# Where the routing coefficient enters the early slots of a two-stage MoE kernel, and where its slot count is read

## The chip, the cores and the metric

One NeuronCore of one Trainium2 chip runs the whole program. The metric is device time in microseconds, a median over executions. Three executions of the kernel before gave 831.27, 835.51 and 840.33 us, so the median is 835.51 us. A profiled execution is one more execution, with its own time.

## The reference

Three parts follow one another, in fp32. Sliding-window attention with 32 global tokens per batch (4 batches, 8 heads, 512 + 32 tokens, head size 64) gives 2176 rows `x` of 512 values, which are 17 tiles of 128 tokens. A SiLU MLP (512 to 2048 to 512) follows. Then comes a mixture of 8 experts in which every token goes to its best expert alone:

```
e_idx  = argmax(x @ w_gate);  gate_w = softmax(x @ w_gate)[e_idx]
eom    = sigmoid(x @ w_output_gate)
h      = relu(x[mask] @ w1[e]);  ye = h @ w2[e]          # w1: 512x1024, w2: 1024x512
out[mask] = gate_w * eom[e] * ye
```

So each output row is the expert's product times one number of the token, `gate_w * eom`.

## The kernel before

Matrix products run in fp16 with each fp32 operand split into a high and a low half (three products for one). The weights of the experts are scaled by a power of two per expert before the split; `i12` holds the inverse scales of the 8 `w1` and the 8 `w2` matrices.

**Slots.** The mixture gathers tokens into slots of 128 rows. Slots 0 to 7 are the early slots: one per expert, filled from the first 15 token tiles, so that their routing is known before the MLP has ended. Slots 8 to 20 are late: `last()` (L1154) computes which expert each has, once the last two token tiles are through. Up to 31 slots can be needed; slots 21 to 30 run inside an `If` at the end (L1560), which reads the number of slots from `eidx` into a register of every engine and compares it. Here 21 slots suffice and the body is skipped.

**Routing.** `last()` ends the list of rows to gather (`idg`, L1188), and then, behind that instruction, computes more: `early_coefs()` (L1137), the rows to scatter to (`ids`, L1201), the experts of the late slots (`eidx`, L1208 and L1209) and the coefficient of every slot's row (`cof`, L1221). `early_coefs` does the work of `cof` a second time for the 8 early slots alone, from 15 token tiles: three DVE products (L1140), 15 small matmuls (L1143), three DVE sums (L1146 to L1148), the expert's inverse scale (L1150, L1151) and their product `cce` (L1152).

**The mixture.** `class Moe` works in 4 chunks of 256 hidden columns. In a chunk every slot gets `mm_h` (L1310: x times w1, relu, split into `hb`, a DMA transpose issued on SP that gives `hT`) and `mm_y` (L1346: `hT` times w2 into PSUM `yp`). In chunk 0, ACT writes `yp` times a column of coefficients into the slot's accumulator `ys` (L1362); in chunks 1 to 3, DVE adds `yp` times the column to `ys` (L1364); in chunk 3 a GpSimd (POOL) indirect DMA then scatters the 128 rows to `out` (L1366). The column is `cce` for early slots evicted before `last()` is through (6 of them, `nye=6`), otherwise `cc`, which `coefs(c)` (L1297) builds once per chunk: `gi` is the product of the inverse scales per expert (L1299, L1300), the late slots take `gi` of their expert times `cof` (L1302 to L1305), the early ones `gi` times `cof` (L1308). The chunk's next weights are loaded, measured and converted between the slots (L925, L228, L961, L962).

Late slots are gathered by POOL (L1258, L1287); the even ones are transposed by DMAs on SP's queue (L1260), half of the rest by TensorE (L1291), into the buffers `woh` and `wol`.

**What sets the order.** Each engine runs its instructions in the order that the Tile planner wrote down at build time: it simulates the timeline with a cost model of its own and gives each engine the instruction that is ready first there. `tc.high_priority` and `tc.issue_after(ins)` bias it; `issue_after` puts what its block traces on the engine of `ins` behind `ins` in that engine's order, without a wait for its completion, and says nothing about other engines. The load of the slot count carries no such order before the change.

Of the kernel before, what the change touches and what calls it, by code (L numbers as in the profile page):

```python
# [9 lines left out]
F32 = mybir.dt.float32  # L10
# [4 lines left out]
ACTF = mybir.ActivationFunctionType  # L15
ALU = mybir.AluOpType
# [10 lines left out]
NE = 8  # L27
# [18 lines left out]
NCH = FE // CH  # L46
KJ = CH // 128
NS = 1
ST = NS * NE
NSLOT = 31  # L50
ND = NSLOT - ST
NMAIN = 21
NEARLY = NE
# [54 lines left out]
def tile_kernel(ctx: ExitStack, tc, csa, csr, q0, q, qn, qg, k0, k, va, vc, w_in, w_out, wg, w1, w2, out, dbg=None):  # L108
    nc = tc.nc
# [872 lines left out]
    eidx = const.tile([128, ND + 1], I32, name="eidx")  # L982
    ohs = const.tile([128, ND, NE], F32, name="ohs")
    idge = const.tile([128, NEARLY], I32, name="idge")
    cce = const.tile([128, NEARLY], F32, name="cce")
    bnd = const.tile([128, 1, NE], F32, name="bnd")

    def route(rt, rps):
        def T(shape, name, dt=F32):
            return rt.tile(shape, dt, name=name)  # L990

        def bc(x, shape):
            return x.to_broadcast(shape)
# [24 lines left out]
        RE = ohb[:, 0:15]  # L1018
# [115 lines left out]
                coef(14, 15)  # L1134
                static(0, 15)

        def early_coefs():  # L1137
            SR = [128, 15, NEARLY]
            for c in range(3):
                DVE.tensor_tensor(Rce[:, :, c], RE, bc(cp[:, c, 0:15], SR), ALU.mult)  # L1140
            pc = rps.tile([128, 3, NEARLY], F32, tag="av", name="pce")
            for i in range(15):
                PE.matmul(pc.rearrange("p c n -> p (c n)"), A[:, i], Rce[:, i].rearrange("p c n -> p (c n)"),  # L1143
                          start=(i == 0), stop=(i == 14))
            v = T([128, 1, NEARLY], "ve")
            DVE.tensor_copy(v[:, 0], pc[:, 2])  # L1146
            DVE.tensor_tensor(v[:, 0], v[:, 0], pc[:, 1], ALU.add)
            DVE.tensor_tensor(v[:, 0], v[:, 0], pc[:, 0], ALU.add)  # L1148
            g = T([128, 1, NE], "ge")
            DVE.tensor_tensor(g[:, 0], i12[:, 0:NE], i12[:, NE:2 * NE], ALU.mult)  # L1150
            DVE.tensor_scalar(g, g, 2.0 ** 19, None, ALU.mult)  # L1151
            DVE.tensor_tensor(cce, v[:, 0], g[:, 0], ALU.mult)  # L1152

        def last():  # L1154
            with tc.high_priority(URG):
                p = onehot(15, 17)
# [30 lines left out]
                        pm_i = PE.matmul(pm, A[:, i], Rc[:, i, c], start=(i == 0 and c == 0), stop=(i == NT - 1 and c == 1))  # L1187
                key_i[0] = DVE.tensor_scalar(idg, pm, -1.0, 0.0, ALU.add, ALU.max)  # L1188
            with tc.issue_after(key_i[0].ins):
                early_coefs()  # L1190
                for c in range(2):
                    DVE.tensor_tensor(Rc[:, :, c], R, bc(row[2 + c], SR), ALU.mult)
                pm = rps.tile([128, NSLOT], F32, tag="av", name="pt")
                for i in range(NT):
                    for c in range(2):
                        PE.matmul(pm, A[:, i], Rc[:, i, c], start=(i == 0 and c == 0), stop=(i == NT - 1 and c == 1))
                ohr = oh.rearrange("p i e -> p (i e)")
                vf = ohr[:, 0:2 * NSLOT].rearrange("p (a n) -> p a n", a=2)
                DVE.tensor_scalar(vf[:, 1], pm, 0.0, float(BIG), ALU.is_equal, ALU.mult)
                DVE.tensor_scalar(vf[:, 1], vf[:, 1], -1.0, None, ALU.add)  # L1200
                DVE.tensor_tensor(ids, vf[:, 1], pm, ALU.add)  # L1201

                SE = [128, ND, NE]
                o2 = tmp.rearrange("p i e -> p (i e)").bitcast(BF16)[:, 0:ND * NE].rearrange("p (n e) -> p n e", e=NE)
                DVE.tensor_tensor(o2, bc(bnd, SE), bc(iota[:, 0:ND].rearrange("p (n a) -> p n a", a=1), SE), ALU.is_le)
                ef = T([128, ND, 1], "ef")
                DVE.tensor_reduce(ef[:, :, 0], o2, AX.X, ALU.add)
                DVE.tensor_scalar(eidx[:, 0:ND], ef[:, :, 0], float(NE - 1), None, ALU.min)  # L1208
                DVE.tensor_copy(eidx[:, ND:ND + 1], bnd[:, 0, NE - 1:NE])  # L1209
                DVE.tensor_tensor(ohs, bc(iota[:, 0:NE].rearrange("p (a e) -> p a e", a=1), SE), bc(ef, SE), ALU.is_equal)  # L1210

                coef(15, 17)
                for c in range(3):
                    DVE.tensor_tensor(Rc[:, :, c], R, bc(cp[:, c], SR), ALU.mult)
                pc = rps.tile([128, 3, NSLOT], F32, tag="av", name="pcf")
                for i in range(NT):
                    PE.matmul(pc.rearrange("p c n -> p (c n)"), A[:, i], Rc[:, i].rearrange("p c n -> p (c n)"),
                              start=(i == 0), stop=(i == NT - 1))
                DVE.tensor_copy(vf[:, 0], pc[:, 2])
                DVE.tensor_tensor(vf[:, 0], vf[:, 0], pc[:, 1], ALU.add)  # L1220
                DVE.tensor_tensor(cof, vf[:, 0], pc[:, 0], ALU.add)  # L1221
# [8 lines left out]
    class Moe:  # L1230
        def __init__(self, slots, ne):
            self.slots, self.ne, self.ns = slots, ne, len(slots)
            self.ev, self.x, self.hT, self.ys, self.hb, self.cc = {}, {}, {}, {}, {}, {}
            self.late, self.xg, self.pair = False, [], [None, None]
            for n, x in enumerate(slots):
                if x < ST:
                    self.ev[n] = x // NS
            o = [z for e in range(0, NE, 2) for k in range(NS) for z in (NE * k + e, NE * k + e + 1)] if ne else []
            self.order = o + list(range(len(o), self.ns))
# [54 lines left out]
            else:  # L1294
                DVE.tensor_copy(x, p)

        def coefs(self, c):  # L1297
            g = cc_p.tile([128, 1, NE], F32, tag="gi", name="gi")
            DVE.tensor_tensor(g[:, 0], i12[:, 0:NE], i12[:, NE:2 * NE], ALU.mult)  # L1299
            DVE.tensor_scalar(g, g, 2.0 ** 19, None, ALU.mult)  # L1300
            t = lg.rearrange("p i e -> p (i e)")[:, 0:ND * NE].rearrange("p (n e) -> p n e", e=NE)
            DVE.tensor_tensor(t, ohs, g.to_broadcast([128, ND, NE]), ALU.mult)  # L1302
            cc = self.cc[c] = cc_p.tile([128, NSLOT], F32, tag="cc", name="cc")
            DVE.tensor_reduce(cc[:, ST:], t, AX.X, ALU.add)
            DVE.tensor_tensor(cc[:, ST:], cc[:, ST:], cof[:, ST:], ALU.mult)  # L1305
            for k in range(NS):
                r = slice(k, ST, NS)
                DVE.tensor_tensor(cc[:, r], cof[:, r], g[:, 0], ALU.mult)  # L1308

        def mm_h(self, n):  # L1310
            x = self.x[n]
# [34 lines left out]
        def mm_y(self, c, n):  # L1346
            s = self.slots[n]
            q, o = divmod(n, 2)
            h = self.hT[q][:, 4 * o:4 * o + 4]
            p, tag = ((ps_x, "x2"), (ps_v, "av"))[n % 2]  # L1350
            ps = p.tile([128, DM], F32, tag=tag, name="yp")
            for m, (hl, l) in enumerate(((0, 0), (0, 1), (KJ, 0))):
                for j in range(KJ):
                    PE.matmul(ps, h[:, hl + j], self.rows("2", n, l, j),  # L1354
                              start=(m == 0 and j == 0), stop=(m == 2 and j == KJ - 1))
            if c == 0:
                if n < self.ne:
                    self.ys[n] = ysv[:, n]
                else:
                    self.ys[n] = self.room(n - self.ne, 1)  # L1360
                cc = self.cc[0][:, s:s + 1] if self.late else cce[:, n:n + 1]
                ACT.activation(self.ys[n], ps, ACTF.Copy, scale=cc)  # L1362
            else:
                DVE.scalar_tensor_tensor(self.ys[n], ps, self.cc[c][:, s:s + 1], self.ys[n], ALU.mult, ALU.add)  # L1364
            if c == NCH - 1:
                ins = POOL.indirect_dma_start(out=out[:, :], out_offset=bass.IndirectOffsetOnAxis(ap=ids[:, s:s + 1], axis=0),  # L1366
                                              in_=self.ys[n], in_offset=None, bounds_check=NTOK - 1, oob_is_err=False)
                tc.declare_no_dep(ins.ins, group="sc", reason="every row is written once")
                tc.add_to_no_dep_group("sc", ins.ins)

        def early(self, ny, i0, i1):
            with tc.issue_after(i0.ins):
                for n in range(2, self.ne):
                    self.mm_h(n)
            with tc.issue_after(i1.ins):
                for n in range(ny):
                    self.mm_y(0, n)
# [44 lines left out]
    with ExitStack():  # L1422
# [134 lines left out]
        ys_p = ctx.enter_context(tc.tile_pool(name="ys", bufs=1))  # L1557
        moe.ys_p, moe.late = ys_p, True
        moe.rest(P["nye"], wq1)
    with tc.If(nc.values_load(eidx[0:1, ND:ND + 1], min_val=0, max_val=ND) > NMAIN - ST):  # L1560
        with ExitStack():
            moe = Moe(list(range(NMAIN, NSLOT)), 0)
            moe.ys_p, moe.late = ys_p, True
            wq = [(0, kd, p) for kd in ("1", "2") for p in range(4)]
            while wpend or wq:
                pump_w(wq)
            moe.rest(0, [(1, "1", p) for p in range(4)])
# [48 lines left out]
```

## Time and profile before

| | us |
|---|---|
| median of three executions | 835.51 |
| the profiled execution | 835.75 |
| its span in the trace | 834.0 |
| TensorE busy in the span | 759.4 (91%) |
| DVE busy | 600.4 (72%) |
| ACT busy | 517.7 (62%) |
| mean granted TensorE clock | 0.973 of full |

The span runs from the first instruction to the last. The profile's chain of waits goes back from the last instruction to whatever released it, step by step. A timeline row gives start, duration, engine, line, operation and tiles; the bracket at its end is the idle time of that engine just before, and what ended it. A name of an engine with a `q` behind it is its instruction queue. The last 270 us or so are the mixture, about 63 us for each of the later chunks.

### The profile page before, as it was taken

How to read it: one execution, taken by the hardware profiler on the slowest of the kernel's cores; microseconds unless marked ns; L12 is line 12 of the kernel's file. 1: busy time of each engine (PE TensorE's matmuls, PEld its weight loads, DVE VectorE, ACT ScalarE, POOL GpSimd, SP SyncE). 2: the span in 40 equal slices, each digit the busy share in tenths (PEclk: the TensorE clock that was granted, in tenths of full speed). 3: DMA queues.
4: the chain of work that ended last, by engine and by line, in shares of the span. 5: the costliest groups of instructions: out<-in, count | busy, mean ns of one | idle time of the engine just before them, and what ended most of it. 6: DMA issues, size and time to landing. Idle time of an engine off the chain costs nothing.

```text
span 834.0 us, 17487 instructions
## 1 busy us (share of the span) xinstructions
PE 759.4 (91%) x6249; PEld 527.4 (63%) x6249; DVE 600.4 (72%) x1653; ACT 517.7 (62%) x1020; POOL 56.8 (7%) x110
## 2 busy tenths in 40 slices
PE   6999949899999989989999989998799798998995
PEld 5998726466776757667766656766566465565552
DVE  4799877767966878747755587749364878878863
ACT  3786667867847758646643895342379666856730
POOL 0000000000000000000000000032300000000144
PEclk9999969999999999999999999999999999999998
DMA  9962552658945475744545865075966746955583
GB/s 321 324 196 88 160 167 102 176 114 195 183 110 74 89 130 119 153 77 77 110 62 103 258 202 153 13 188 131 201 134 189 228 83 171 258 109 165 151 186 104
DMA packets 176235, 126.25 MB, mean 151 GB/s; under 512 B 155149, under 2 KB 156941, under 8 KB 172944
## 3 DMA queue, kind: packets, MB, share of 16 engines
q1 hardware_dynamic: 172784, 115.10, 56.7%
q0 software_dynamic: 3360, 9.97, 4.2%
q8 instruction: 54, 0.88, 0.4%
q14 instruction: 37, 0.30, 0.1%
HBM read 76.93 MB, written 9.96 MB: 104 GB/s over the span
## 4 chain that ended last, share of the span: by engine, by line
PE 41%; DMA 12%; DVE 7%; ACT 5%; issue 3%; SPq 1%; POOLq 0%; ACTq 0%; DVEq 0%
PE h L688 9%; PE x L735 9%; PE yp L1354 9%; PE hp L1325 6%; DMA ws<-in_w_dram 5%; DMA pT<-pb 4%; PE hp L1317 2%; PE av L538 2%; DMA wil<-hb 1%; DVE w1b L962 1%; ACT w1b L961 1%; DMA woh<-yx 1%; PE hp L1320 1%; ACT junk L228 1%; ACT w2b L961 1%
## 5 line engine op out<-in xcount | busy, mean ns | idle before, releaser
L735 PE MATMUL x<-woh,g 128*128 128x512 f16 x544 | 172.3, 379 | 3.5 <-ACT g L718 1.5
L688 PE MATMUL h<-xT,wih 128*128 128x256 f16 (+1 forms) x1152 | 160.4, 271 | 10.1 <-DMA xT<-xb 4.9
L735 PEld LDWEIGHTS <-g 128*128 128x128 f16 x816 | 76.4, 98 | 85.3 <-issue 2.7
L688 PEld LDWEIGHTS <-wih 128*128 128x128 f16 x1152 | 108.1, 100 | 34.2 <-DMA xT<-xb 5.2
L1354 PE MATMUL yp<-w2b,wil 128*128 (+1 forms) x384 | 93.7, 391 | 11.0 <-ACT w2b L961 5.3
L735 PE MATMUL x<-wol,g 128*128 128x512 f16 x272 | 103.1, 379 | 0.0
L688 PE MATMUL h<-xT,wil 128*128 128x256 f16 (+1 forms) x576 | 88.0, 272 | 0.0
L690 ACT ACTIVATE tanh<-h,th 128x512 f32<-128x512 f32 (+1 forms) x72 | 47.2, 658 | 64.0 <-PE h L688 61.4
L470 ACT ACTIVATE e<-e,mx,esc 128x192 f32<-128x192 f32 (+1 forms) x128 | 70.1, 549 | 18.5 <-DVE mx L467 15.5
L1354 PEld LDWEIGHTS <-wil 128*128 128x128 f16 x384 | 38.1, 103 | 51.4 <-DMA wil<-hb 8.4
L707 ACT ACTIVATE g<-tanh,i_out 128x512 f16<-128x512 f32 (+1 forms) x64 | 44.1, 691 | 33.3 <-DVE tanh L703 33.2
L228 ACT ACTIVATE junk<-ws 128x1024 f16<-128x1024 f32 x48 | 50.4, 1052 | 17.4 <-DMA ws<-in_w_dram 17.2
L466 DVE CUSTOM_DVE_ANT_0 e<-s,cs 128x192 f32<-128x192 f32 (+1 forms) x128 | 42.5, 367 | 23.2 <-PE s L455 10.4
L688 PEld LDWEIGHTS <-wil 128*128 128x128 f16 x576 | 54.4, 100 | 7.4 <-issue 0.5
L708 DVE SCALAR_TENSOR_TENSOR g<-tanh,i_out,g 128x512 f16<-128x512 f32 (+1 forms) x64 | 45.6, 713 | 17.0 <-ACT g L707 16.9
L703 DVE SCALAR_TENSOR_TENSOR tanh<-tanh,h 128x512 f32<-128x512 f32 (+1 forms) x64 | 41.4, 649 | 21.3 <-ACT tanh L690 21.0
L962 DVE SCALAR_TENSOR_TENSOR w1b<-ws,s,w1b 128x1024 f16<-128x1024 f32 x32 | 40.4, 1280 | 17.2 <-ACT w1b L961 17.0
L1325 PE MATMUL hp<-w1b,x 128*128 128x256 f16 x384 | 48.7, 279 | 1.2 <-ACT r L1338 1.2
L1325 PEld LDWEIGHTS <-x 128*128 128x128 f16 x384 | 38.6, 102 | 10.7 <-issue 2.1
L523 DVE SCALAR_TENSOR_TENSOR pb<-e,pb 128x384 f16<-128x384 f32 (+1 forms) x48 | 27.6, 586 | 22.9 <-ACT pb L522 22.8
L962 DVE SCALAR_TENSOR_TENSOR w2b<-ws,s,w2b 128x1024 f16<-128x1024 f32 x32 | 40.2, 1280 | 2.6 <-ACT w2b L961 2.6
L1364 DVE SCALAR_TENSOR_TENSOR yx<-yp,cc,yx 128x512 f32<-128x512 f32 x39 | 29.1, 748 | 8.9 <-PE yp L1354 8.8
(361 smaller groups left out, 1447.6 us busy)
## 6 DMA issues: line engine op xcount, KB each, us to landing
ws<-in_w_dram SPq DMA_DIRECT2D x64, 512.0 KB, 4.5
st<-in_w_out_dram SPq DMA_DIRECT2D x8, 1024.0 KB, 5.0
st<-in_w_in_dram SPq DMA_DIRECT2D x6, 1024.0 KB, 12.0
q<-in_q_dram SPq DMA_DIRECT2D x12, 512.0 KB, 4.0
x2d<-x2s SPq DMA_DIRECT2D x17, 256.0 KB, 2.7
st<-in_k_dram SPq DMA_DIRECT2D x3, 1088.0 KB, 7.0
st<-in_qn_dram SPq DMA_DIRECT2D x3, 1024.0 KB, 5.1
st<-in_va_dram SPq DMA_DIRECT2D x3, 1024.0 KB, 6.9
```

Source lines behind the costliest of these rows:

```text
L228: ACT.activation(junk, x, ACTF.Square, accum_out=m)
L466: DVE.tensor_tensor_reduce(dst[:, hh, 0:wt], ps[:, hh, 0:wt], mask, 1.0, -3e38, ALU.add, ALU.max, mx[:, hh:hh + 1])
L470: ACT.activation(dst[:, hh, 0:wt], dst[:, hh, 0:wt], ACTF.Exp, scale=esc[:, b:b + 1], bias=mx[:, 2 + hh:3 + hh], accum_out=sums[i][:, h:h ...
L688: PE.matmul(ps[:, f], w[:, kk, c], xj[:, l + kk, 0:n], start=(m == 0 and kk == 0), stop=(m == 2 and kk == KD - 1))
L690: pin[0] = ACT.activation(t, ps, ACTF.Tanh, scale=th[:, b:b + 1])
L703: pin[1] = DVE.scalar_tensor_tensor(t, t, 1.0, ps, ALU.add, ALU.mult)
L707: ACT.activation(hi, t, ACTF.Copy, scale=i)
L708: pin[2] = DVE.scalar_tensor_tensor(lo, t, i, hi, ALU.mult, ALU.subtract)
L735: PE.matmul(x2ps[2 * j + c], x[:, f, o], w[:, ff], start=(ff == 0 and m == 0), stop=(ff == KF - 1 and m == 2))
L962: DVE.scalar_tensor_tensor(d[:, 1], t[a], sc_, d[:, 0], ALU.mult, ALU.subtract)
L1325: PE.matmul(ps[:, 0], x[:, xl + kk], self.rows("1", n, l, kk), start=(m == 0 and kk == 0), stop=(m == 2 and kk == KD - 1))
L1354: PE.matmul(ps, h[:, hl + j], self.rows("2", n, l, j), start=(m == 0 and j == 0), stop=(m == 2 and j == KJ - 1))
```

## The change

`early_coefs` and `cce` are gone. A new method `scales` makes `gi` alone, and `early` calls it for chunk 0. Early slots are evicted with their column of `gi` in every chunk; after chunk 3's addition one ACT instruction per early slot multiplies `ys` by the slot's column of `cof` in place, and the scatter follows. `coefs` makes the columns of the late slots only. The load of the slot count is put behind the last scatter in POOL's order.

```diff
         with tc.issue_after(key_i[0].ins):
-                early_coefs()
...
-        def coefs(self, c):
-            g = cc_p.tile([128, 1, NE], F32, tag="gi", name="gi")
+        def scales(self, c):
+            g = self.gi[c] = cc_p.tile([128, 1, NE], F32, tag="gi", name="gi")
             DVE.tensor_tensor(g[:, 0], i12[:, 0:NE], i12[:, NE:2 * NE], ALU.mult)
             DVE.tensor_scalar(g, g, 2.0 ** 19, None, ALU.mult)
+
+        def coefs(self, c):
+            if c not in self.gi:
+                self.scales(c)
+            g = self.gi[c]
...
-            for k in range(NS):
-                r = slice(k, ST, NS)
-                DVE.tensor_tensor(cc[:, r], cof[:, r], g[:, 0], ALU.mult)
...
-                cc = self.cc[0][:, s:s + 1] if self.late else cce[:, n:n + 1]
+                cc = self.gi[0][:, 0, n:n + 1] if n < self.ne else self.cc[0][:, s:s + 1]
                 ACT.activation(self.ys[n], ps, ACTF.Copy, scale=cc)
             else:
-                DVE.scalar_tensor_tensor(self.ys[n], ps, self.cc[c][:, s:s + 1], self.ys[n], ALU.mult, ALU.add)
+                cc = self.gi[c][:, 0, n:n + 1] if n < self.ne else self.cc[c][:, s:s + 1]
+                DVE.scalar_tensor_tensor(self.ys[n], ps, cc, self.ys[n], ALU.mult, ALU.add)
+            if c == NCH - 1 and n < self.ne:
+                ACT.activation(self.ys[n], self.ys[n], ACTF.Copy, scale=cof[:, s:s + 1])
             if c == NCH - 1:
                 ins = POOL.indirect_dma_start(out=out[:, :], ...)
...
+                self.end = ins
 
         def early(self, ny, i0, i1):
+            self.scales(0)
...
-    with tc.If(nc.values_load(eidx[0:1, ND:ND + 1], min_val=0, max_val=ND) > NMAIN - ST):
+    with tc.issue_after(moe.end.ins):
+        more = nc.values_load(eidx[0:1, ND:ND + 1], min_val=0, max_val=ND)
+    with tc.If(more > NMAIN - ST):
```

## Rows read from the trace of the kernel before

**Rows 1.** The page's head.
```profile
span 834.0 us, 17487 instructions
```

**Rows 2.** The page's chain of waits, shares of the span by engine.
```profile
PE 41%; DMA 12%; DVE 7%; ACT 5%; issue 3%; SPq 1%; POOLq 0%; ACTq 0%; DVEq 0%
```

**Rows 3.** Timeline of the end, all engines: start, duration, engine, line, operation.
```profile
822.86 0.75 DVE L1364 SCALAR_TENSOR_TENSOR yx<-yp,cc,yx 128x512 f32<-128x512 f32 x1 [0.55 <-PE yp L1354]
823.88 0.97 POOL L1366 DMA_INDIRECT out_dram<-yx,ids  x1 [0.33 <-DVE yx L1364]
824.15 0.75 DVE L1364 SCALAR_TENSOR_TENSOR yx<-yp,cc,yx 128x512 f32<-128x512 f32 x1 [0.54 <-PE yp L1354]
829.54 0.97 POOL L1366 DMA_INDIRECT out_dram<-yx,ids  x1 [4.68 <-DMA out_dram<-yx,ids]
```

**Rows 4.** Line 1560: durations in ns (min/median/max), first and last start.
```profile
L1560 SPq TENSOR_LOAD <-eidx x1: 1665/1665/1665, 586.0 to 586.0; - x1
...
L1560 ACTq COMPARE_BRANCH  x1: 50/50/50, 811.9 to 811.9; - x1
...
L1560 ACTq EVENT_SEMAPHORE  x1: 17/17/17, 815.7 to 815.7; - x1
...
L1560 PEldq COMPARE_BRANCH  x1: 3807/3807/3807, 821.1 to 821.1; - x1
L1560 POOLq TENSOR_LOAD <-eidx x1: 487/487/487, 823.6 to 823.6; - x1
...
L1560 POOLq COMPARE_BRANCH  x1: 45/45/45, 824.2 to 824.2; - x1
...
L1560 POOLq INC_SWDGE_SEM  x1: 579/579/579, 828.1 to 828.1; - x1
```

**Rows 5.** Line 1366, the scatters: from issue to landing.
```profile
DMA to landing us min/median/max: 2.5/3.3/6.0
```

**Rows 6.** Line 1612, the program's end, on POOL's queue.
```profile
L1612 POOLq DRAIN  x3: 40/113/3825, 829.3 to 833.7; - x3
```

**Rows 7.** Timeline around the end of the routing, all engines.
```profile
575.96 2.75 PE L1354 MATMUL yp<-w2b,wil 128*128 128x512 f16 x12
...
581.13 0.15 DVE L1152 TENSOR_TENSOR cce<-ve,ge 128x8 f32<-128x8 f32 x1
...
581.38 1.26 ACT L1362 ACTIVATE wih<-yp,cce 128x512 f32<-128x512 f32 x2 [1.59 <-DVE gw L1075]
...
582.58 1.47 PE L1354 MATMUL yp<-w2b,wil 128*128 128x512 f16 x6 [2.64 <-ACT wih L1362]
...
594.15 0.93 PE L1325 MATMUL hp<-w1b,woh 128*128 x5 [3.96 <-DMA woh<-yx]
...
594.88 2.76 PE L1354 MATMUL yp<-w2b,wil 128*128 128x512 f16 x6
...
598.68 1.03 PE L1317 MATMUL hp<-w1b,woh 128*128 x4
```

**Rows 8.** The chain of waits in order of time: start, duration, what.
```profile
584.29 9.73 DMA woh<-yx
...
795.80 5.96 DMA wil<-hb
```

**Rows 9.** Stretches: length, busy time of each engine, granted clock, DMA share.
```profile
590.20:594.10 3.90, 0.00 (x0) 0.04 (x1) 0.85 (x2) 0.80 (x2) 2.37 (x3) 1.00 1.04 173
...
594.70:598.20 3.50, 3.50 (x16) 1.74 (x15) 0.00 (x0) 0.51 (x1) 0.00 (x0) 0.51 1.04 221
```

**Rows 10.** The same view in chunk 3, early slots' last additions (PE, PEld, DVE, ACT, POOL).
```profile
786.00:801.00 15.00, 14.23 (x90) 8.57 (x88) 14.52 (x34) 6.77 (x15) 8.76 (x8) 1.00 0.59 144
```

**Rows 11.** Groups by line and shape: busy us, mean ns of one.
```profile
L1362 ACT ACTIVATE wih<-yp,cce 128x512 f32<-128x512 f32 x6 | 4.0, 686 | 11.9 <-PE yp L1354 10.3 <-DVE gw L1075 1.6
L1140 DVE TENSOR_TENSOR ohs<-ohb,cp 128x120 bf16<-128x120 bf16 x3 | 0.7, 279 | 0.0
L1308 DVE TENSOR_TENSOR cc<-cof,gi 128x8 f32<-128x8 f32 x4 | 0.6, 158 | 0.0
L1364 DVE SCALAR_TENSOR_TENSOR wih<-yp,cc,wih 128x512 f32<-128x512 f32 x24 | 16.9, 743 | 0.8 <-PE yp L1354 0.8
```

More of the change, by code (lines that the diff above doesn't have):

```diff
@@ L984, in tile_kernel @@
     idge = const.tile([128, NEARLY], I32, name="idge")
-    cce = const.tile([128, NEARLY], F32, name="cce")
     bnd = const.tile([128, 1, NE], F32, name="bnd")
@@ L1135, in early_slots @@
                 static(0, 15)
[L1137 to L1152, printed above, removed]
         def last():
@@ L1232, in __init__ @@
             self.slots, self.ne, self.ns = slots, ne, len(slots)
-            self.ev, self.x, self.hT, self.ys, self.hb, self.cc = {}, {}, {}, {}, {}, {}
+            self.ev, self.x, self.hT, self.ys, self.hb, self.cc, self.gi = {}, {}, {}, {}, {}, {}, {}
             self.late, self.xg, self.pair = False, [], [None, None]
```

## The prediction

> **What bounds the kernel now.** I read the page first. The span is 834.0 us [rows 1], and the profiled execution took 835.75, so 1.75 us lie outside the span; its time stands 0.24 us above the median of 835.51. Sums are made against 835.75. The chain of waits [rows 2] belongs to PE for 41%, then to DMA (12%): TensorE sets the pace, broken by short stretches in which it waits for something. So an edit is worth what it does at a stretch where PE waits, or at the very end. I then looked at the three places that the change touches.
>
> **The end.** In the timeline [rows 3] each late slot's addition on DVE is followed by its scatter on POOL. The last but one ends at 822.86 + 0.75 = 823.61 and its scatter starts at 823.88, 0.27 later. The last addition ends at 824.90, yet its scatter starts at 829.54. The reader is to see that 4.4 us are lost there, and the trace names a DMA for it. Line 1560's rows [rows 4] show more: POOL's load of the slot count stands at 823.6, its branch at 824.2, and POOL's next instruction at 828.1, 3.9 us on, 0.58 long. So POOL's queue went through the load and the `If` before it took the last scatter. The gap is not POOL's alone: ACT has 3.8 us from its branch (811.9) to its next instruction (815.7), and PE's branch lasts 3.81.
>
> **The routing's end.** In [rows 7] PE finishes two early slots' y products (12 matmuls) and later waits 2.64 us, until 582.58, for ACT's evictions, which began at 581.38 because `cce` came at 581.13. Then PE waits again, 3.96 us until 594.15, for the transposed rows of a late slot: that DMA is on the chain for 9.73 us from 584.29 [rows 8] and the DMA engines are full there (share 1.04, [rows 9]). Behind that wait stand, in PE's order, the y products of the sixth early slot (594.88, 6 matmuls) and at 598.68 the first h products of slot 9, which TensorE had transposed itself and which needs no such DMA.
>
> **Chunk 3, early slots.** From 786 to 801 DVE is busy 14.52 of 15 us, ACT 6.77 [rows 10]: DVE is full, ACT has 8.2 us free.
>
> **The change, part by part.** *Load behind the last scatter.* Moved are POOL's load, and through its register the branch and what follows. The last scatter starts 0.27 behind the last addition: 824.90 + 0.27 = 825.17 instead of 829.54. The load now starts when the queue has passed that scatter, about 824.9 (before: 823.6, as the last but one was released at 823.61). With the distances of [rows 4], branch 0.6 later at 825.5, next instruction 3.9 later at 829.4, 0.58 long: 830.0. Before, POOL's drain ended at 829.3 + 3.8 = 833.1 [rows 6], 3.6 behind the start of the last scatter and 0.9 ahead of the end. Now that scatter allows 825.17 + 3.6 = 828.8, so the branch comes last: 830.0, plus up to 0.6 as between 828.7 and the drain's start at 829.3, plus 0.9 is 831.2. **Gain 2.8 us.** Bounds: if the branch cost nothing the whole 4.4 comes back; if the scatter takes the longest landing of [rows 5], 6.0 instead of the median 3.3, it ends 2.7 later, at 831.5, and the span at 832.4, gain 1.6. I take 2.8, since four engines' distances are the nearest rows. [...] The loads of the other four engines are not tied to anything: SP's, 1.67 us long at 586.0 among the late slots' transposes [rows 4], may stay or go. The transposes there wait on full DMA engines, so I count 0, with 1.7 as its bound either way.
>
> *No `cce`.* Removed from DVE are 3 products of 0.28 and six small instructions of about 0.16 [rows 11], some 1.8 us (`gi` was made before as well), and 15 small matmuls. They stand ahead of `cce` and delay nothing else that PE waits for. What counts is the wait for `cce`: `gi` depends on the weights alone, so ACT can evict the first y product when it ends, near 577.5, and PE's 2.64 us go. What is late next is the DMA that lands at 594.0; nothing here brings it forward. So PE arrives sooner and waits longer, and the gain is only the work that moves from behind 594.15 to ahead of it. The sixth early slot's y products wait for nothing new and are the likeliest: 6 of the 12 matmuls of 2.75 us at 575.96, at full clock, so **1.4 us**, which I take. Low end 0 (order unchanged). [...]
>
> [...]
>
> *Columns.* `coefs` loses one DVE instruction of 0.16 us in each chunk, and the 24 additions of early slots [rows 11] wait for `gi` alone. In chunk 3 DVE is full, so 0.16 may count; I take 0, bounds 0 and 0.6 gained. *Eight multiplications on ACT.* Each is like L1362's, 0.69 us [rows 11] (reading SBUF, not PSUM, so an estimate): 5.5 us in all. They lie between an addition on DVE and a scatter on POOL. Behind them on ACT stand the relu copies and `hb` halves of late slots. ACT's 8.2 free us cover them, and early scatters end 20 us ahead of the last one: I take 0. Low 0, high 5.5 with no cover.
>
> Sum: 835.75 - 2.8 - 1.4 = **831.5 us**.
>
> **Rivals.** *A, PE's second wait fills.* With buffers free sooner, slot 9 and 11 run ahead of slot 10. For it: they need no SP transposes. Against: PE's order is fixed at build, and the order of before left them behind. [...]
> *B, the routing's end gives nothing.* The 2.64 us are moved into the wait at 594. For it: DMA share 1.04. [...]
> *C, slower: ACT takes DVE's lateness.* The place is ACT's order from 786 to 801. A multiplication that waits for a DVE addition holds the `hb` halves behind it, their transposes on SP, and so the y products of late slots, for which PE already waits on a 5.96 us transpose [rows 8]. It decides from the point where ACT's free 8.2 us no longer fall between additions. Price up to 5.5: 835.75 - 2.8 + 5.5 = 838.5, slower than before.
> *D, the move does nothing*, because POOL's `If` is still planned ahead of that scatter: against it, the branch needs the register that the moved load fills. 834.4.
>
> **Numbers.** Chances: forecast 0.47, A 0.2, B 0.17, C 0.13, D 0.03. A measurement of this kernel tells about 1% from no change, 8.4 us here: faster means under 827.2, slower over 843.9. A reaches the first line only at its end, and a re-planned order may add a little: 0.17. Beyond the other line only C with a worse order lies: 0.07. Same: 0.76. The range takes A's end and nearly C's: 826.5 to 838.
>
> **What would show it.** The last scatter 0.3 us behind the last addition, and POOL's branch behind it; the span's end some 6 us behind the last addition, not 9. No PE wait for ACT near 580; the sixth early slot's products ahead of the wait for the late slot's rows. ACT idle between 786 and 801 still over 2 us, and PE's wait for the transpose there no longer than before. I am wrong if the end moves by less than 1.5 us, if PE's waits between 576 and 600 sum to as much as before with the same work left, or if that transpose comes later by more than 2 us.

## The result, and the profile after

The changed kernel takes 826.49 us (median of 6 runs, 825.20 to 828.53); the kernel before, run on the same chip beside it, 837.32. The ratio is 0.988 [0.984, 0.992], a gain of 1.2%, some 10 us. (The ratios leave out runs that were disturbed, so here and below they are not quite the quotients of the medians; the profile of e_nopin is of such a run.) The forecast was 831.5, a gain of 4.2 us by its sum: the sign is right, the size is not, and the time lies at the very edge of the range, whose lower end was 826.5. So the question is where the other 6 us came from.

The profiled execution took 825.91. The page's head and its chain of waits, which answer to [rows 1, 2]:

```profile
span 824.1 us, 17447 instructions
...
PE 43%; DMA 10%; DVE 5%; ACT 4%; issue 4%; POOL 0%; SPq 0%; POOLq 0%; ACTq 0%; DVEq 0%
```

The span is 9.9 us shorter. To see where, I cut both traces at four events that both have: the first `pm` product of the routing, TensorE's last y product of chunk 0, its last one of chunk 1, its last one of chunk 3, and then the stretch from the end of the last addition on DVE. The stretches of before (from:to and length; busy us of PE, PEld, DVE, ACT, POOL with instructions; granted clock; DMA share; GB/s):

```profile
575.10:643.40 68.30, 61.26 (x493) 39.83 (x491) 36.23 (x113) 42.24 (x76) 12.91 (x13) 0.98 0.81 174
643.40:699.70 56.30, 51.80 (x312) 30.43 (x311) 44.38 (x100) 37.77 (x65) 0.00 (x0) 0.97 0.60 160
699.70:824.10 124.40, 113.44 (x702) 69.38 (x700) 96.50 (x219) 70.13 (x127) 19.66 (x20) 0.97 0.69 170
824.90:834.00 9.10, 0.00 (x0) 0.00 (x0) 0.00 (x0) 0.00 (x0) 0.97 (x1) 0.61 0.13 49
```

The same of after:

```profile
575.40:641.00 65.60, 60.80 (x479) 39.38 (x477) 34.98 (x101) 42.31 (x76) 13.08 (x13) 0.97 0.84 180
641.00:699.30 58.30, 52.91 (x310) 30.62 (x310) 45.89 (x105) 38.01 (x66) 0.00 (x0) 0.94 0.66 164
699.30:816.60 117.30, 110.57 (x703) 67.83 (x700) 94.24 (x213) 74.54 (x133) 20.76 (x20) 1.00 0.70 177
817.40:824.10 6.70, 0.00 (x0) 0.00 (x0) 0.02 (x1) 0.00 (x0) 0.97 (x1) 0.70 0.18 66
```

The reader is to see that the third row holds most of it: chunks 2 and 3 take 7.1 us less for the same 702 or 703 matmuls. In that row PE is busy 2.9 us less and idle 4.2 us less (124.40 - 113.44 = 11.0 against 6.7). The end gives 2.4, the routing 2.7, and chunk 1 takes back 2.0.

**The end.** After's timeline (start, duration, engine, line, operation), which answers to [rows 3]:

```profile
816.67 0.75 DVE L1348 SCALAR_TENSOR_TENSOR yx<-yp,cc,yx 128x512 f32<-128x512 f32 x1 [0.54 <-PE yp L1337]
817.70 0.97 POOL L1352 DMA_INDIRECT out_dram<-yx,ids  x1 [0.33 <-DVE yx L1348]
```

The last scatter starts 0.28 us behind the last addition (817.42), where before it was 4.64. The rows of the `If` in after (ns min/median/max, first and last start), which answer to [rows 4]:

```profile
L1550 POOLq EVENT_SEMAPHORE  x4: 17/43/2412, 818.2 to 818.4; - x4
...
L1550 ACTq COMPARE_BRANCH  x1: 50/50/50, 803.1 to 803.1; - x1
...
L1550 ACTq EVENT_SEMAPHORE  x1: 17/17/17, 806.3 to 806.3; - x1
...
L1550 POOLq COMPARE_BRANCH  x1: 45/45/45, 818.0 to 818.0; - x1
...
L1550 POOLq INC_SWDGE_SEM  x1: 595/595/595, 820.9 to 820.9; - x1
```

POOL's branch now stands behind the last scatter, and 2.8 us lie between it and POOL's `INC_SWDGE_SEM` (`INC` from here on). But 2.41 of them are a wait on a semaphore, from 818.44 to 820.85. The chain of before says for what (start, duration, what):

```profile
823.88 4.69 DMA out_dram<-yx,ids
828.57 0.10 POOLq L1560
```

By it, POOL's queue waits there until the scatter that it had issued last has landed. The landing signals themselves agree: the last one of that scatter comes at 828.07 in the trace and `INC` starts at 828.10; in after the last scatter's comes at 820.83 and the wait ends at 820.85. (The chain's 828.57 already lies inside `INC`.) Of before, I had read the 3.9 us behind POOL's branch as the price of the branch, because ACT (3.8 us) and PE (3.81) show as much at theirs.

**The routing's end.** PE's timeline in after, which answers to [rows 7]:

```profile
576.22 2.75 PE L1337 MATMUL yp<-w2b,wil 128*128 128x512 f16 x12
...
579.67 1.46 PE L1337 MATMUL yp<-w2b,wil 128*128 128x512 f16 x6
584.25 1.25 PE L1198 MATMUL pcf<-wil,A 128*128 128x93 bf16 x17 [3.12 <-DVE wil L1195]
585.29 4.12 PE L1337 MATMUL yp<-w2b,wil 128*128 128x512 f16 x12
...
590.08 1.46 PE L1337 MATMUL yp<-w2b,wil 128*128 128x512 f16 x6
...
594.57 1.23 PE L1308 MATMUL hp<-w1b,woh 128*128 x8 [1.68 <-DMA woh<-yx]
```

PE no longer waits for ACT, and all six early slots stand ahead of the wait for the late slot's rows. But it now waits 3.12 us for the operand of the coefficients' product, a wait of 0.4 us before.

**Chunks 2 and 3.** PE's timeline of before around the first y product of chunk 3:

```profile
767.89 1.47 PE L1325 MATMUL hp<-w1b,x 128*128 128x256 f16 x12 [0.69 <-ACT r L1338]
771.99 0.83 PE L1354 MATMUL yp<-w2b,wil 128*128 128x512 f16 x2 [2.63 <-ACT w2b L961]
...
775.19 2.03 PE L1325 MATMUL hp<-w1b,x 128*128 128x256 f16 x15
```

And of after:

```profile
768.81 1.47 PE L1308 MATMUL hp<-w1b,x 128*128 128x256 f16 x12 [0.63 <-ACT r L1321]
771.63 1.47 PE L1337 MATMUL yp<-w2b,wil 128*128 128x512 f16 x6 [1.35 <-DMA wil<-hb]
...
773.23 1.02 PE L1300 MATMUL hp<-w1b,woh 128*128 x4
```

Before, PE comes to slot 0's y product too early and waits 2.63 us for the chunk's weights, which ACT is still converting; chunk 2 has the same wait, 2.66. The stretches behind the two waits in before:

```profile
710.80:714.20 3.40, 3.40 (x18) 2.42 (x17) 1.16 (x6) 2.68 (x5) 0.00 (x0) 0.50 1.00 356
...
772.20:775.60 3.40, 3.14 (x10) 1.31 (x9) 3.14 (x10) 2.53 (x7) 0.00 (x0) 0.50 0.98 377
```

And in after behind the waits that stand there now, 1.22 and 1.35 us:

```profile
711.00:714.40 3.40, 3.40 (x19) 1.71 (x18) 3.20 (x10) 2.22 (x6) 0.00 (x0) 1.00 1.27 257
...
771.60:775.00 3.40, 3.37 (x19) 1.78 (x20) 3.25 (x10) 3.00 (x7) 0.00 (x0) 1.00 1.07 291
```

The granted clock (column before the DMA share) was 0.50 for 3.4 us behind each wait of before, and stays at 1.00 in after. By an estimate from these rows, half of 3.4 us, that is up to 1.7 us lost twice. PE's busy time, which holds this loss, is 2.9 us less in after; the 4.2 us of idle time are the rest of the 7.1.

Why does PE come later to that product? The two programs differ in the order that was written out for TensorE, in places that the diff doesn't touch (h3.5 is the h product of slot 5 in chunk 3, y3.0 the y product of slot 0 there):

```
before  h3.3 h3.4 h3.5 y3.0 h3.6 h3.7 h3.8 y3.2 ...
after   h3.3 h3.4 h3.5 h3.6 h3.7 y3.0 h3.8 h3.9 y3.2 ...
before  ... h2.13 h2.14 h2.15 y2.8
after   ... h2.15 h2.16 h2.17 h2.18 h2.19 h2.20 y2.8
```

The h products of slots 6 and 7 stand ahead of slot 0's y product and fill the time in which its weights are made. The late slots' first y product moved behind the last h product, in chunks 1 and 2.

The first of these two is not enough by itself. Three of the kernels below (e_nocce, e_col, e_force8) have slot 0's y product behind slot 7's h products in chunk 2, but in chunk 1 slot 8's y product begins where before has it. Their chunk 2 takes 63.2 to 64.2 us, as in the kernels with before's order (63.1 to 63.8) and not as in those with after's (60.4 to 61.3). They wait in another place: for `tot`, a small product with which the next weights' size is measured (L192, from ACT's L228), 2.3 to 3.7 us, with half clock behind it (in e_col 0.50 for 3.4 us, from 709.5). e_col's row, and after's in the same place:

```profile
707.88 0.38 PE L192 MATMUL tot<-mw,cr 128*128 128x2 f32 x2 [2.26 <-ACT junk L228]
...
704.49 0.38 PE L192 MATMUL tot<-mw,cr 128*128 128x2 f32 x2 [0.86 <-ACT junk L228]
```

So by these runs the gain of a chunk needs the new order of its own start together with that of the late y products of the chunk before. e_force8's chunk 3, which has both by hand (of the late slots only slot 8's is held), has the gain. Why both are needed is not shown beyond that wait.

### The profile page after: what moved, and what is told of

The parts are those of the page before. It is cut to its first block, busy times and chain, and to the rows that moved or that the text cites. A ratio compares the mean times of both kernels' runs of the same rounds, so it can differ in the third digit from the quotient of the medians.

```text
span 824.1 us, 17447 instructions
## 1 busy us (share of the span) xinstructions
PE 758.7 (92%) x6234; PEld 526.8 (64%) x6234; DVE 598.7 (73%) x1640; ACT 522.3 (63%) x1028; POOL 58.4 (7%) x110
## 4 chain that ended last, share of the span: by engine, by line
PE 43%; DMA 10%; DVE 5%; ACT 4%; issue 4%; POOL 0%; SPq 0%; POOLq 0%; ACTq 0%; DVEq 0%
PE x L735 10%; PE h L688 10%; PE yp L1337 10%; PE hp L1308 5%; DMA ws<-in_w_dram 3%; DMA pT<-pb 3%; PE hp L1300 2%; PE av L538 2%; DMA wil<-hb 2%; PE hp L1303 1%; ACT w1b L961 1%; DMA woh<-yx 1%; DVE w1b L962 1%; ACT junk L228 1%; DMA yx<-x2d,idg 1%
## 5 line engine op out<-in xcount | busy, mean ns | idle before, releaser
L470 ACT ACTIVATE e<-e,mx,esc 128x192 f32<-128x192 f32 (+1 forms) x128 | 70.1, 549 | 18.3 <-DVE mx L467 15.4
L228 ACT ACTIVATE junk<-ws 128x1024 f16<-128x1024 f32 x48 | 50.5, 1052 | 17.6 <-DMA ws<-in_w_dram 17.6
L521 POOL MEMSET pb<- 128x256 f16 (+1 forms) x48 | 12.4, 258 | 328.6 <-DMA pT<-pb 143.6
```

The costliest lines, as they stand in the source:

```text
L228: ACT.activation(junk, x, ACTF.Square, accum_out=m)
L470: ACT.activation(dst[:, hh, 0:wt], dst[:, hh, 0:wt], ACTF.Exp, scale=esc[:, b:b + 1], bias=mx[:, 2 + hh:3 + hh], accum_out=sums[i][:, h:h ...
```

## The experiments

Each ratio is against the kernel before, run on the same chip beside it. There were three chips: e_pin, e_nocce, e_gicol and e_nopin on the first (before there: 839.07), e_wait, e_force8, e_noscale and e_col on the second (845.67), the rest on the third (843.93). The forecasts in us were made against 837 to 839 for the kernel before and 826.5 for after, so on the slower second chip they are to be read as ratios.

**e_pin: the load alone.** The kernel before, with only this:

```diff
-    with tc.If(nc.values_load(eidx[0:1, ND:ND + 1], min_val=0, max_val=ND) > NMAIN - ST):
+    with tc.issue_after(moe.end.ins):
+        more = nc.values_load(eidx[0:1, ND:ND + 1], min_val=0, max_val=ND)
+    with tc.If(more > NMAIN - ST):
```

> The kernel before with one edit: the load of the slot count put behind the last scatter in POOL's order. Theory 1 (the end is worth what the trace after shows: 9.1 us from the last addition to the end of the span before, 6.7 after; the other 7.5 us of the change come from elsewhere): the last scatter starts 0.3 us behind the last addition, the span ends 6 to 7 us behind that addition, and the time is 2.4 us under the kernel before's (837.3), 834.9; the mixture's PE waits stay as before. Rival (moving the load also re-plans the order and is the source of most of the change): under 831.

835.94 us, ratio 0.9995 [0.9955, 1.0036]. Its trace shows the mechanism in full: the last scatter 0.27 us behind the last addition, the span's end 6.6 behind it, not 9.1. Its ratio doesn't show it: 2.4 us are 0.3%, and the interval is 0.4% to each side. So the end term stands by the trace, and the load alone is not what made the kernel faster by 1.2%.

**e_nocce: no `cce` alone.** The kernel before, chunk 0 by `gi`, chunks 1 to 3 by `cc`, no multiplications on ACT:

```diff
-                early_coefs()
...
-                cc = self.cc[0][:, s:s + 1] if self.late else cce[:, n:n + 1]
+                cc = self.gi[0][:, 0, n:n + 1] if n < self.ne else self.cc[0][:, s:s + 1]
```

> The kernel before without early_coefs and cce: the first additions of the early slots (chunk 0) use the inverse scales alone, chunks 1 to 3 use the columns of cc as before, there is no multiplication at the end and the load of the slot count is not moved. The early slots' output lacks the coefficient in chunk 0's part. Theory 1 (removing cce re-plans TensorE's order in chunks 2 and 3 as well, so that it no longer waits 2.6 us before the first y products there and the clock no longer falls): 5 to 7.5 us under the kernel before (837.3), 830 to 832, with two stretches of half clock instead of four in the mixture. Theory 2 (those chunks gain because the additions of early slots wait for gi and not for cc): only the routing's end gains, 1 to 2.5 us, 835 to 836, and four stretches of half clock.

830.69 us, ratio 0.9932 [0.9886, 0.9978]. That is Theory 1's time without its mechanism: TensorE's order of chunk 3 is exactly before's, and chunks 2 and 3 take 124.5 us in the trace, with a half-clock stretch in each (granted clock 0.97 over both, as in before). Near 580 PE waits 3.0 us for the operand of the coefficients' product, in place of the wait for ACT. Where the 0.7% come from the trace does not show.

**e_gicol: the columns alone.** The kernel before, `cce` kept:

```diff
-                DVE.scalar_tensor_tensor(self.ys[n], ps, self.cc[c][:, s:s + 1], self.ys[n], ALU.mult, ALU.add)
+                DVE.scalar_tensor_tensor(self.ys[n], ps, self.gi[c][:, 0, n:n + 1] if n < self.ne else self.cc[c][:, s:s + 1], self.ys[n], ALU.mult, ALU.add)
```

> The kernel before with the early slots' additions of chunks 1 to 3 taking the inverse scales alone as their column; cce stays for chunk 0, the load is not moved, nothing is multiplied at the end. The early slots' output lacks the coefficient in the parts of chunks 1 to 3. Theory 1 (order re-planned by the removal of cce): no gain, 836 to 838. Theory 2 (the wait for cc is what chunks 2 and 3 lost): 4 to 6 us under the kernel before (837.3), 831 to 833.

838.27 us, ratio 1.0005 [0.9953, 1.0057]: that early additions wait for `gi` alone gains nothing by itself that shows at 0.5%.

**e_nopin: the change without the moved load.** The kernel after, with the load where it was:

```diff
-    with tc.issue_after(moe.end.ins):
-        more = nc.values_load(eidx[0:1, ND:ND + 1], min_val=0, max_val=ND)
-    with tc.If(more > NMAIN - ST):
+    with tc.If(nc.values_load(eidx[0:1, ND:ND + 1], min_val=0, max_val=ND) > NMAIN - ST):
```

> The changed kernel with the load of the slot count left where the planner puts it. Theory 1: the last scatter stands behind the If again, 4 us behind the last addition, the span ends 9 us behind it, 2.4 us over the changed kernel (826.5): 829. Rival (the planner puts the load behind the last scatter by itself once the order has changed): 826.5.

829.27 us, ratio 0.988 [0.975, 1.001]; the interval is wide, from 4 runs. In its trace the last scatter is 3.5 us behind the last addition again and the end 8.0. With e_pin: most of the gain is not at the end.

**e_wait: the wait for `cce` put back.** The kernel after, in which the first six evictions take their scale from a copy that DVE makes only behind the routing's `ids`:

```diff
+            with tc.issue_after(i2.ins):
+                DVE.tensor_scalar(cce, self.gi[0][:, 0], 1.0, None, ALU.mult)
...
-                cc = self.gi[0][:, 0, n:n + 1] if n < self.ne else self.cc[0][:, s:s + 1]
+                cc = cce[:, n:n + 1] if n < P['nye'] and self.ne else self.gi[0][:, 0, n:n + 1] if n < self.ne else self.cc[0][:, s:s + 1]
```

> The changed kernel with the wait for the routing put back without its work: the first evictions of the six early slots take a copy of the inverse scales that DVE makes behind the list of rows to scatter to. TensorE's order in chunks 2 and 3 is that of the changed kernel. Theory O (the change gains through TensorE's order in chunks 2 and 3: the first y product there stands behind the h products of slot 7, not of slot 5, and slot 8's behind all h products): PE waits 2 to 3 us for an eviction near 580 again, and the time is within 2 us of the changed kernel's 826.5. Theory M (the eviction wait in the routing was worth most of it): 831 or more.

833.67 us, ratio 0.984 [0.977, 0.990]. PE waits for ACT again (13.6 us, on a chip where other kernels wait as long there for something else, see the last section), and the kernel gains as much as the change. That fits a wait worth nothing, within 0.6%. It is a weak test, though: on this chip PE stands for 12.6 and 13.6 us near 580 also in e_noscale and e_col, which lack the wait that was put back, so that wait can be hidden in the longer stop.

**e_noscale: no multiplications at the end.** The kernel after without these lines:

```diff
-            if c == NCH - 1 and n < self.ne:
-                ACT.activation(self.ys[n], self.ys[n], ACTF.Copy, scale=cof[:, s:s + 1])
```

> The changed kernel without the eight ACT multiplications in chunk 3; the early slots' output lacks the coefficient. TensorE's order is the changed kernel's but for chunk 3's end. Forecast in the prediction: they cost 0, so 826 to 827. Rival C of the prediction (ACT holds the late slots' halves): up to 5.5 us faster, 821 to 824.

836.58 us, ratio 0.986 [0.978, 0.993], no better than e_wait beside it, which has them. With these two intervals the times alone could hardly show 5.5 us (0.65%); what the trace of after says of the multiplications stands in the next section.

**e_col: the columns put back.** The kernel after, in which early additions take their scale from `cc` again, by one DVE instruction in each chunk:

```diff
+            if self.ne:
+                DVE.tensor_tensor(cc[:, 0:ST], cr[:, C_ONE:C_ONE + NE], g[:, 0], ALU.mult)
...
-                cc = self.gi[c][:, 0, n:n + 1] if n < self.ne else self.cc[c][:, s:s + 1]
+                cc = self.cc[c][:, s:s + 1]
```

> The changed kernel with the early slots' column of chunks 1 to 3 copied into cc by one DVE instruction per chunk, as before, so that their additions wait for it. TensorE's order in chunk 3 falls back to that of the kernel before, in chunk 2 half. Theory O: half of the gain of those chunks is lost, 3 to 5 us over the changed kernel, 829.5 to 831.5. Rival (the order there is worth nothing, and 0.16 us per chunk is all): 826.5 to 827.2.

841.29 us, ratio 0.995 [0.992, 0.998]: more than half of the gain is lost, more than Theory O's half, for one small instruction in each chunk. Its program has before's order in chunk 3, and the old wait with it (PE's timeline):

```profile
773.88 0.63 PE L1339 MATMUL yp<-w2b,wil 128*128 128x512 f16 x2 [2.64 <-ACT w2b L961]
...
777.06 4.79 PE L1310 MATMUL hp<-w1b,x 128*128 128x256 f16 x24
```

**e_force8: the kernel before, its order changed by hand in chunks 2 and 3.** Slot 0's y product is held behind slot 7's h product, and slot 8's behind the last h (`hi[n]` is the last h matmul of slot n):

```diff
-                                self.mm_y(c, n)
+                                held = {0: self.hi[7], 8: self.hi[self.ns - 1]}.get(n) if self.ne and c > 1 else None
+                                with tc.issue_after(held.ins) if held else ExitStack():
+                                    self.mm_y(c, n)
```

> The kernel before, with cce, cc and the load as they were, and one thing ordered: in chunks 2 and 3 slot 0's y product stands behind slot 7's h products on TensorE and slot 8's behind the last slot's. Theory O: 5 to 8 us under the kernel before (839 over its many runs), 831 to 834; the 2.65 us waits ahead of the first y products are under 1.5 us. Theory M, or columns: no gain, 837 to 840.

842.22 us, ratio 0.995 [0.991, 0.999]: part of the gain from order alone, and less than Theory O's forecast. Chunk 1 was still planned as in before; chunk 2 takes 64.2 us and keeps its half-clock stretch (719.1; granted clock 0.99 over chunks 2 and 3), behind a wait of 3.73 us for `tot`. Chunk 3, ahead of which slot 8's y product was held too, takes 57.5 us, where before has 61.2 and after 56.9.

**e_full: before's arithmetic in after's order.** The kernel before with e_pin's load and

```diff
+                                held = None if not (self.ne and c) else self.hi[7] if n == 0 else self.hi[self.ns - 1] if n >= self.ne and c < 3 else None
+                                with tc.issue_after(held.ins) if held else ExitStack():
+                                    self.mm_y(c, n)
```

> The kernel before with cce, cc and its four columns untouched, and two orders given by hand: on TensorE, in chunks 1 and 2 every late slot's y product stands behind the last slot's h products, and in chunks 1 to 3 slot 0's y product behind slot 7's h products; on POOL, the load of the slot count stands behind the last scatter. TensorE's order of h and y products from chunk 2 on is then that of the changed kernel. Theory O (the order on TensorE and the end are the whole gain): a ratio to the kernel before of 0.985 to 0.991, as the changed kernel. Rival D (the data flow matters: early columns that wait for nothing but the inverse scales): 0.993 to 0.996, as the runs that had the order or the end only in part.

838.21 us, ratio 0.992 [0.988, 0.996]. This lies between the forecasts of Theory O and rival D, and the interval reaches into both; the trace decides. `cce`, the columns and the coefficients are all as before; h and y products stand as in after in chunk 2 and in chunk 3 up to slot 4's y product. The stretch of chunks 2 and 3:

```profile
712.90:830.10 117.20, 109.98 (x703) 68.05 (x700) 94.99 (x217) 69.41 (x125) 18.90 (x18) 1.00 0.71 178
```

**e_colf: e_col in the same order by hand.** Both edits on the kernel after:

```diff
+                DVE.tensor_tensor(cc[:, 0:ST], cr[:, C_ONE:C_ONE + NE], g[:, 0], ALU.mult)
...
+                held = None if not (self.ne and c) else self.hi[7] if n == 0 else self.hi[self.ns - 1] if n >= self.ne and c < 3 else None
```

> The changed kernel with the early columns of chunks 1 to 3 copied into cc, which alone gave 0.9947, and TensorE's order given by hand as in the last kernel. Theory O: the gain comes back, 0.985 to 0.990. Rival D: it stays at 0.993 to 0.996.

834.65 us, ratio 0.987 [0.982, 0.992], Theory O's and below rival D's: what e_col lost comes back with the order, its extra instructions still there. Its stretch of chunks 2 and 3, ahead of it e_col's:

```profile
701.40:828.70 127.30, 116.85 (x705) 70.44 (x703) 96.78 (x216) 75.78 (x135) 17.62 (x18) 0.96 0.64 166
```

```profile
705.60:823.70 118.10, 110.40 (x703) 67.98 (x700) 94.24 (x216) 74.78 (x133) 18.80 (x18) 1.00 0.69 174
```

**e_after: the change again**, on the third chip, unedited.

> The changed kernel once more, beside the others on their chip. Both theories: 0.984 to 0.992 of the kernel before.

833.39 us, ratio 0.989 [0.984, 0.994].

**e_aft8: after, with slot 8's y product behind the last h in chunk 3 too.** e_force8's edit on the kernel after:

```diff
+                held = {0: self.hi[7], 8: self.hi[self.ns - 1]}.get(n) if self.ne and c > 1 else None
```

> The changed kernel with slot 8's y product of chunks 2 and 3 behind the last slot's h products; only chunk 3 changes by it. Theory O says nothing of this place; if y products that stand ahead of h products wait there for DMA transposes, 0 to 2 us under the changed kernel, otherwise the same within 1 us; the last h products' transposes come earlier, so no loss is expected.

835.37 us, ratio 0.991 [0.986, 0.996]: no better than after. None of these kernels is faster than after by more than the intervals allow.

The length of the stretch of chunks 2 and 3 in all profiles, us, by the order of its program:

| order of chunks 2 and 3 | kernels | us | granted clock |
|---|---|---|---|
| slot 0's first y product in chunk 3 as in before | before, e_pin, e_gicol, e_nocce, e_col | 124.4, 125.7, 123.2, 124.5, 127.3 | 0.97, 0.95, 0.97, 0.97, 0.96 |
| slots 0 and 8 held by hand | e_force8 | 121.8 | 0.99 |
| as after (e_noscale but for chunk 3's end) | after, e_nopin, e_wait, e_noscale, e_after | 117.3, 119.2, 119.6, 118.3, 119.1 | 1.00 in all |
| as after, in part by hand | e_full, e_colf, e_aft8 | 117.2, 118.1, 117.5 | 1.00 in all |

The first group's mean is 125.0, that of the eight with after's order 118.3, and the groups don't meet, although the runs come from several chips. The order is worth 6.7 us in this stretch. Chunk 1, cut in the same way, costs about 1.1 of that: 57.1 in the mean of the six kernels in which slot 8's y product begins where before has it, 58.2 in that of the eight others; there the two groups overlap (56.2 to 58.0, 57.2 to 59.3).

## Why the prediction came out as it did

The time fell into the range by luck: the lower end of the range was there for rival A, which did not happen (PE still waits 1.68 us for slot 10's rows, and slot 9's products stand behind them). More than half of the gain came from a place that the sum put at nothing.

*Load behind the last scatter, -2.8: the size came, by luck; the reason was wrong.* Measured 2.4 in the two profiles, inside the bounds 1.6 to 4.4. The places came as foretold: scatter 0.28 behind the addition, branch 0.6 behind that addition, end 6.70 behind it where the step gave 6.3. What holds the end was named wrongly. I took the 3.9 us behind POOL's branch for a price of the branch, and `INC` for POOL's next instruction. It is not the next; before has four others ahead of it:

```profile
L1560 POOLq EVENT_SEMAPHORE  x4: 17/43/43, 824.4 to 825.2; - x4
```

POOL goes on 0.2 us behind its branch; what it then waits for is the landing of the scatter ahead of it. So the moved load can't save that wait, it only makes the last scatter start ahead of it: 817.70 plus 3.15 until the wait ends, 0.6 for `INC`, 1.8 for the drain and 0.8 behind it give the span's end. Two errors of the sum cancelled: it had 3.9 us from the branch to `INC`, which took 2.9, and no time for the drain, which took 1.8. (Its last step, 830.0 plus up to 0.6 plus 0.9, gives 830.9 to 831.5; 831.2 is the middle.) In the six profiles of before, after and the first chip, the last addition stands 8.0 to 9.1 us ahead of the end without the move and 6.6 and 6.7 with it, so the term is 1.3 to 2.5 us. ACT has 3.2 us from its branch (803.1) to its next instruction (806.3), with no wait in between that the profile shows; what fills them is not shown, and they lie off the path. The branches themselves take 45 ns on POOL and 50 ns on ACT.

*No `cce`, -1.4: the order came, the gain didn't.* ACT's wait went and the sixth early slot moved ahead, but PE then waited 3.12 us at the coefficients' product (`pcf`), which DVE's chain feeds. I had said that the DMA of 594 was late next; `pcf` was. PE's waits between 575 and 600 sum to 4.8 us, before to 7.0. From `pm`, a product of the routing, to chunk 0's last y product after took 2.7 us less, yet the same stretch takes 64.8 to 69.7 in three kernels that share before's program there, on chips without the long wait, and 65.6 and 70.1 in after and e_nopin. So these traces can't tell a gain of 1.4 us from none, and e_wait, whose chip hides the wait, doesn't decide it. Rival B's reading, nothing gained, fits both; e_nocce's 0.7% speaks against it. As for the clock there, one stretch of 3.4 us at a granted clock of 0.50 stands in after (from 584.6), as one at 0.51 does in before (from 594.7). The lower end of the range takes PE's wait as wholly filled, 3.96 us, and adds 1.7 us for the clock. No run shows that 1.7: in after 1.68 us of the wait are left, and half clock takes as long as before; in e_after the granted clock is 0.61 from 587.9 to 591.4.

*Eight multiplications on ACT, 0: right.* The stretch of after that answers to [rows 10]:

```profile
781.50:796.50 15.00, 15.00 (x90) 8.55 (x89) 13.13 (x30) 10.40 (x20) 9.16 (x8) 1.00 0.58 144
```

Each multiplication took 0.72 us, where the estimate had 0.69. ACT still has 4.6 us free, and PE is busy throughout: the wait for the late slot's transpose that rival C feared has gone. e_noscale is no faster without them, which agrees, as far as its interval reaches.

*Columns, 0 with bounds 0 to 0.6: this term was mis-sized, and it is the step that failed.* It counted what additions wait for, with the program otherwise as it was. But the order of every engine is planned from the work and its costs, so that an edit re-plans all that lies behind it. With `cce` and the columns both gone, the plan put two h products ahead of slot 0's y product in chunks 2 and 3, and the late slots' y products later in chunks 1 and 2. That is worth 6.7 - 1.1 = 5.6 us, and with the end's 2.4 it makes 8.0, 0.96% of 837 us, inside the measured 0.8 to 1.6%. Neither edit does it alone (e_gicol, e_nocce: stretch as before); e_col takes most of it away with one small instruction in each chunk, e_colf gives it back by order alone, and e_full has most of it with none of the change's arithmetic. Under rival A I had written that PE's order is fixed at build and left things behind; it is fixed, but not the same in the two builds, and I had ended with "a re-planned order may add a little".

*Left open.* Whether the 0.4% between e_full and after is real: their intervals overlap. Why e_nocce is 0.7% faster than before (0.2 to 1.1%), when its trace shows the old length in chunks 2 and 3; its one profile is of a run 2.6 us over its median and e_pin's of one 5.7 us under, so single traces don't resolve this. Until that is known, a share of `cce` in the gain is not excluded; e_full, with `cce`, bounds it at what lies between its ratio and after's.

## What to carry to other kernels

Where a planner writes the order, a small edit has two effects, its own and that of the new plan, and the second can be the larger one and lie far from the edit: compare the order of the two programs before crediting the arithmetic. The test is to force the new order on the old kernel by hand, and the old operation on the new one. And a long time behind a branch is to be followed to its waits on each engine by itself; that other engines show the same length is no proof of the same cause.

## What the runs showed of the hardware that I had not expected

On the second and third chip PE stops for 10 to 14 us near 580, where those of before and after and the four of the first chip have 2.5 to 3.2. In e_after on the third (all engines' timeline):

```profile
584.24 0.19 DVE L1180 TENSOR_SCALAR oh<-pt 128x31 f32<-128x31 f32 x1 [8.45 <-remote]
...
587.13 0.69 ACT L1345 ACTIVATE wih<-yp,gi 128x512 f32<-128x512 f32 x1 [11.55 <-remote]
...
587.94 1.49 PE L1198 MATMUL pcf<-wil,A 128*128 128x93 bf16 x17 [11.02 <-DVE wil L1195]
```

DVE and ACT both stood still for 8 us and more, while POOL issued the late slots' gathers one behind the other. The view doesn't name the releaser ("remote"), but the trace has it: both wait for a semaphore that TensorE updates. The update behind its last `pt` product (a product of the routing, whose result DVE's L1180 reads) comes at 584.21, 8.6 us behind the end that the profile models for the product (575.62); in after it comes 0.02 us behind (579.84 and 579.82). So the stop begins at TensorE, between that product and its signal; DVE and ACT wait for it, and PE's 11.02 us follow from DVE's. The lag is 8.6 to 11.8 us in seven of the eight kernels profiled on these two chips and at most 0.05 in the six others. Its cause is open. PE's stop stands in every kernel profiled on those chips, two of them (e_force8, e_full) with before's order on TensorE up to the end of chunk 0, so the ratios should hold; before itself was not profiled there.

In the same profile the last scatter comes 3.07 us behind the last addition, although the load is behind it: DVE's additions had come late and then in a bunch, five in 3.39 us from 815.69; POOL's scatters followed each other 1.28 us apart, and were behind until the end. The end was 9.4 us behind the last addition there, no better than in before. Counted from TensorE's last product, the seven kernels with the moved load on these chips have 9.3 to 10.2 us to the end and e_force8, without it, 11.4; in the six other profiles it is 7.4 and 7.5 with it and 8.7 to 9.9 without. So the move seems to keep its worth of one to two us, but the distances themselves don't carry from chip to chip.
